# Reordering the opening loads of an attention-and-FFN block, with the second tile's statistics on ScalarE and half the keys turned late

## The chip, the cores and the metric

The kernel runs on one core of a Trainium2 chip. The metric is the device time of one execution in microseconds (us).

## The reference

One block of a transformer whose layernorms are modulated by a conditioning vector `c` (S = 2048 tokens, D = 1024, 32 query heads and 4 key heads of 128, 512 keys, then a gated FFN of width 3584):

```python
mod = (_silu(c) @ w_mod).reshape(c.shape[0], 6, 1, -1)
sa, ca, ga, sb, cb, gb = ...                      # six rows of 1024
h = _layernorm(x) * (1 + ca) + sa                 # scale ca, shift sa
x = x + ga * attention(h, k_cache, v_cache, wq, wo)   # last 512 keys only
h = _layernorm(x) * (1 + cb) + sb
x = x + gb * ffn(h)
```

The change touches only how the first line for `h` and the first heads of the attention get under way.

## The kernel before

TensorE, VectorE, ScalarE and GpSimd run at once and hand buffers over by semaphores that a small recorder (`T.op`) places. The opening works on the first 512 tokens (four tiles of 128) and does this: load four token tiles, the columns of `w_mod` for the scale `ca`, query weights, keys, the columns for the shift `sa`, values; normalize the tiles; transpose them on TensorE (`open_turn`), copy them out of PSUM (`open_evict`), multiply by 1 + ca (`open_scale`); project the first six heads (`q_open` for heads 0 to 3 on 256 tokens at a time, `q_more` for heads 4 and 5); turn the keys on TensorE; make the shift row from 8 x 8 one-column matmuls (`shift_column`); and from it one shift per head (`shifts`), which is added as the query leaves PSUM (`q_shifted`). Then come the scores of head 0 and the loop over heads.

The loads, as issued:

```python
for t in range(TPC): load_x(t)          # 4 x 256 KB
load_ca(0)                              # scale weights, half of the columns: 4 x 256 KB
load_wq(0, (0,))                        # query group 0, half of the rows: 512 KB
load_ca(1)
load_wq(0, (1,))
T.op(Q_k, ... k_nat ...)                # all keys: 512 KB
load_wq(1)                              # query group 1: 2 x 512 KB
load_sa()                               # shift weights: 8 x 256 KB
for gk in range(Hkv): ...               # values: 4 x 128 KB
```

The keys, and the end of the opening:

```python
def turn_keys():
    for i in range(GK):                 # 16
        b = (QBK, XBK)[i // 8]
        transpose(bank_bf(b)[...], k_nat[...], P, [B_kn], PB[b])
    for j in range(2):
        T.op(DVE, lambda: V.tensor_copy(kT[:, 8 * j:8 * j + 8, :], ...), ...)

turn_keys()
q_more(4, range(DT))                    # head 4: 8 matmuls of 512 columns
for kc in range(6):
    shift_column(kc)
    if kc > 3:
        keep_warm(1, XBK)               # a matmul whose result nobody reads
shift_column(6)
keep_warm(2, XBK)
shift_column(7)
T.op(DVE, lambda: V.tensor_copy(sa, bank(SFT, DT)), ...)
shifted_input(0)
q_more(5, range(3))
shifts([0], XBK)
q_more(5, [3])
... # shifts([1, 2]), q_more(5, 4..5), shifts([3, 4, 5]), q_more(5, 6..7), six q_shifted, eight shifted_input
scores(0)
exps(0, 2)
```

And the step of the head loop that weights the values. `between` runs after the matmuls and ahead of the reciprocal:

```python
def pv(i, between):
    for kt in range(KT):
        for j in (0, 2, 1, 3):
            mm(bank(...), ex[es][:, kt, ...], v_sb[...], ...)      # 128 x 129
    between()
    T.op(DVE, lambda: V.reciprocal(rl, den), ...)
    T.op(DVE, lambda: V.tensor_tensor(o_sb[...], num, rl_bc, ALU.mult), ...)
```

The softmax here doesn't subtract the row's maximum and nothing guards it: scores larger than these inputs give would overflow.

Of the kernel before, what the change touches and what calls it, by code (L numbers as in the profile page):

```python
# [8 lines left out]
P = 128  # L9
# [109 lines left out]
def bass_adaLN_cond__sliding_block_cached__swiglu_ffn__prompt_kernel(  # L119
# [104 lines left out]
    for i in (2, 3):  # L224
        xsum[i], B_xsum[i] = small("xsum%d" % i, 3, F32)
    shift, B_shift = small("shift", 6, F32)
    B_shift = [B_shift, _Buf("shift1"), _Buf("shift3")]
    SHIFTS = (0, 1, 1, 2, 2, 2)
# [33 lines left out]
    with nc.Block() as block:  # L262

        @block.gpsimd
        def _(g):
# [13 lines left out]
            for t in range(TPC):  # L279
                load_x(t)  # L280
# [12 lines left out]
            def load_sa():  # L293
                for kc in range(DT):
                    T.op(Q_wm[DT + kc], lambda: SP.dma_start(wm[:, DT + kc, :], w_mod[kc * P:(kc + 1) * P, 0:D]), writes=[B_sw[kc]])
# [7 lines left out]
            def load_wq(gi, halves=(0, 1)):  # L303
# [4 lines left out]
                for j in halves:  # L308
# [6 lines left out]
            load_wq(0, (0,))  # L315
            load_ca(1)
            load_wq(0, (1,))
            B_kn = _Buf("kn")
            k_nat = M.take(AT_MS * KB, [Hkv, KT * P], BF16, [B_kn])
            Q_k, Q_v = dq("q_k"), dq("q_v")  # L320
            T.op(Q_k, lambda: SP.dma_start(k_nat, A_k_cache[0, :, Sk - W:Sk, :].rearrange("g (p k) d -> p g (k d)", k=KT)),
                 writes=[B_kn])
            load_wq(1)
            load_sa()
# [9 lines left out]
            for gk in range(Hkv):  # L334
                T.op(Q_vg[gk], lambda: SP.dma_start(
                    v_sb[:, gk * KT:(gk + 1) * KT, 0:P],
                    A_v_cache[0, gk, Sk - W:Sk, :].rearrange("(p k) d -> p k d", k=KT)), writes=[B_vg[gk]])

            def hd(i):

                p = i % Hq
# [117 lines left out]
            TBK = (OBK, OBK + 1, SCB[1], OBK + 1)  # L459
# [9 lines left out]
            def scale_done(half):  # L469
# [3 lines left out]
                T.op(DVE, lambda: V.tensor_copy(g1f[:, lo:hi], g1[:, lo:hi]), reads=[B_g1h[half]], writes=[B_g1f])  # L473
# [11 lines left out]
            def open_evict(tt):  # L485
                b = TBK[tt]
                dst = h_sb[1][:, :, tt * P:(tt + 1) * P]
                src = bank_bf(b)[:, 0:DT * P].rearrange("p (a b) -> p a b", a=DT)
                if tt == 2:
                    T.op(ACT, lambda: A.activation(dst, src, AF.Copy), writes=PB[b] + [B_hn[1][tt]])  # L490
                else:
                    T.op(DVE, lambda: V.tensor_copy(dst, src), writes=PB[b] + [B_hn[1][tt]])  # L492

            def open_scale(th, kc, st=DVE):
                x_ = h_sb[1][:, kc, 256 * th:256 * th + 256]
                rd = B_hn[1][2 * th:2 * th + 2]
# [6 lines left out]
            Q0 = [SCB[0], SCB[2], SCB[3], OBK, OBK + 1, QBK]  # L503

            def q_open(i, kcs, th):

                for kc in kcs:
                    mm(bank(Q0[i], 256, 256 * th), wq_sb[0][:, kc, hd(i) * P:(hd(i) + 1) * P], h_sb[1][:, kc, 256 * th:256 * th + 256],
                       kc == 0 and th == 0, kc == DT - 1, [B_wq[0][kc // 4], B_o[th][kc]], PB[Q0[i]], loose=True)

# [19 lines left out]

            keep_warm(7)
# [3 lines left out]
            sums_1(2)  # L535
            ln_stats(1, 1, 0)
            ln_norm(0, 0, n0[0], B_n0[0])
            ln_stats(1, 1, 1)
            ln_rstd(1)
            sums_1(3)  # L540
            open_turn(0)
            open_evict(0)
            keep_warm(2)
            scale_column(0, 0)
            keep_warm(3)
            scale_column(0, 1)
            keep_warm(2)
            ln_norm(1, 1, n0[1], B_n0[1])
            sums_2(2)
            scale_column(0, 2)  # L550
            keep_warm(1)
            open_turn(1)
            open_evict(1)
            scale_column(0, 3)
            scale_done(0)
            keep_warm(2)
            sums_2(3)
            for kc in range(4):
                open_scale(0, kc)
            ln_norm(2, 2, n0[2], B_n0[2])  # L560
            q_open(0, range(4), 0)
            q_open(1, range(4), 0)
            open_turn(2)
            open_evict(2)
            ln_norm(3, 3, n0[3], B_n0[3])
            q_open(2, range(4), 0)
            q_open(3, range(4), 0)
            open_turn(3)
            open_evict(3)
            scale_column(1, 0)  # L570
            scale_column(1, 1)
            for kc in range(4):
                open_scale(1, kc, ACT if kc == 3 else DVE)
            scale_column(1, 2)
            scale_column(1, 3)
            scale_done(1)
            for i in range(4):
                q_open(i, range(4), 1)
            for th in range(2):
                for kc in range(4, 8):  # L580
                    open_scale(th, kc, ACT if kc > 5 else DVE)
            for th in range(2):
                for i in range(4):
                    q_open(i, range(4, 8), th)
# [37 lines left out]
            def turn_keys():  # L622
                for i in range(GK):
                    b = (QBK, XBK)[i // 8]
                    transpose(bank_bf(b)[:, (i % 8) * P:(i % 8 + 1) * P], k_nat[:, i // KT, (i % KT) * P:(i % KT + 1) * P], P,
                              [B_kn], PB[b])
                for j in range(2):
                    T.op(DVE, lambda: V.tensor_copy(kT[:, 8 * j:8 * j + 8, :],
                                                    bank_bf((QBK, XBK)[j])[:, 0:8 * P].rearrange("p (a b) -> p a b", a=8)),
# [968 lines left out]
```

## Time and profile before

| | before |
|---|---|
| time, median of 3 runs | 1168.09 us |
| span of the profiled execution | 1165.9 us |
| first query matmul | 12.01 us |
| last shift weight landed | 26.25 us |
| scores of head 0 | 29.83 to 30.69 us |
| weighted values of head 0 / head 4 start | 32.68 / 43.70 us |
| from the start of head 4 to the end | 1122.2 us |

The columns of the timeline are start in us, length in us, engine, source line and operation, out<-in with the form, number of instructions, and in brackets the idle time ahead and what ended it.

### The profile page before, as it was taken

What the parts mean: (1) busy time and instruction counts of PE and PEld (TensorE: products, weight loads), DVE (VectorE), ACT (ScalarE), POOL (GpSimd) and SP (SyncE); (2) the same over time, 40 slices, a digit from 0 to 9 for tenths busy, and PEclk for the clock granted to TensorE, in tenths of its full rate; (3) what the DMA queues carried; (4) which work ended last, traced back from release to release, by engine and by line L of the source; (5) the groups of instructions that cost most, each with busy time, mean ns of one, the idle gap of its engine ahead of it and who ended that gap; (6) DMA issues with size and microseconds to landing.
All of it is one profiled execution on the core that took longest, in us unless ns stands there. A gap on an engine that the chain in (4) does not pass through costs nothing.

```text
span 1165.9 us, 20810 instructions
## 1 busy us (share of the span) xinstructions
PE 1146.7 (98%) x7789; PEld 669.7 (57%) x7907; DVE 786.7 (67%) x1718; ACT 526.2 (45%) x844; POOL 21.7 (2%) x41
## 2 busy tenths in 40 slices
PE   8999999999999999999999999999999999999998
PEld 5787645777548876468864444444444444444443
DVE  4888646877638877347847688888377777776214
ACT  3777503777217775057751244444110344444110
POOL 1000000000000000000000000000010000000000
PEclk9999999999999999999999999999999999999999
DMA  9999796999859997869949765666895232322733
GB/s 289 246 250 260 203 357 231 262 272 257 268 202 284 272 218 210 306 149 287 272 99 349 247 176 182 206 180 175 276 246 179 86 86 77 105 73 65 261 126 135
DMA packets 283876, 245.57 MB, mean 211 GB/s; under 512 B 109952, under 2 KB 247168, under 8 KB 283776
## 3 DMA queue, kind: packets, MB, share of 16 engines
q1 hardware_dynamic: 253328, 179.74, 58.3%
q10 hardware_dynamic: 30448, 64.50, 15.6%
q8 instruction: 63, 1.03, 0.4%
q14 instruction: 37, 0.30, 0.1%
HBM read 189.27 MB, written 30.41 MB: 188 GB/s over the span
## 4 chain that ended last, share of the span: by engine, by line
PE 95%; DMA 2%; DVE 1%; ACT 1%; issue 1%; POOL 0%; DVEq 0%; ACTq 0%
PE ps L267 95%; DMA arena<-in_A_wo_dram 1%; ACT arena L758 1%; DMA arena<-arena 0%; PE ps L271 0%; DVE arena L775 0%; ACT arena L1025 0%; DMA arena<-in_c_dram 0%; ACT arena L742 0%; DVE arena L977 0%; DVE arena L492 0%; DVE arena L372 0%; DVE arena L707 0%; DVE arena L774 0%; DVE arena L980 0%
## 5 line engine op out<-in xcount | busy, mean ns | idle before, releaser
L267 PE MATMUL ps<-arena 128*128 128x512 bf16 (+5 forms) x7740 | 1144.3, 308 | 13.4 <-DVE arena L500 1.2
L267 PEld LDWEIGHTS ps<-arena 128*128 128x128 bf16 (+1 forms) x7858 | 666.9, 98 | 488.4 <-issue 6.8
L758 ACT ACTIVATE arena<-ps 128x1024 bf16<-128x1024 f32 x256 | 262.0, 1027 | 37.6 <-PE ps L267 34.8
L644 DVE TENSOR_TENSOR arena<-arena 128x512 f16<-128x512 bf16 (+3 forms) x510 | 223.1, 481 | 26.5 <-DMA wo_sums<-arena 13.5
L703 ACT ACTIVATE arena<-ps 128x256 f32<-128x256 f32 x180 | 68.7, 382 | 136.7 <-PE ps L267 136.2
L1304 DVE TENSOR_TENSOR arena<-ps,arena 128x512 f16<-128x512 f32 x112 | 77.3, 690 | 40.0 <-PE ps L267 37.9
L1297 ACT ACTIVATE arena<-ps 128x512 f32<-128x512 f32 x112 | 66.9, 597 | 73.6 <-PE ps L267 73.6
L707 DVE TENSOR_TENSOR arena<-ps,arena 128x256 bf16<-128x256 f32 x180 | 75.8, 421 | 32.6 <-PE ps L267 30.4
L775 DVE TENSOR_TENSOR arena<-ps,arena 128x512 bf16<-128x512 f32 x128 | 88.5, 692 | 4.5
L1326 ACT ACTIVATE ps<-ps 128x512 f32<-128x512 f32 x56 | 32.6, 582 | 119.7 <-PE ps L267 119.4
L977 DVE TENSOR_TENSOR arena<-ps,arena 128x512 f32<-128x512 f32 x34 | 23.4, 689 | 87.7 <-PE ps L267 87.6
L774 DVE RECIPROCAL arena<-ps 128x4 f32<-128x4 f32 x128 | 23.2, 181 | 52.5 <-PE ps L267 52.4
L1316 DVE TENSOR_TENSOR arena<-ps,arena 128x512 bf16<-128x512 f32 x56 | 38.6, 688 | 29.7 <-ACT arena L1311 29.7
L1311 ACT ACTIVATE arena<-ps 128x512 f16<-128x512 f32 x56 | 33.3, 595 | 31.6 <-PE ps L267 31.6
L980 DVE TENSOR_TENSOR arena<-ps,arena 128x512 bf16<-128x512 f32 x22 | 15.2, 689 | 46.0 <-PE ps L267 46.0
L428 DVE BATCH_NORM_STATS2 arena<-arena 128x6 f32<-128x512 bf16 x56 | 38.4, 687 | 9.1 <-DMA arena<-x_mid 8.8
L1008 DVE SCALAR_TENSOR_TENSOR arena<-arena 128x512 f32<-128x512 bf16 x56 | 41.6, 743 | 0.1
L1311 ACT ACTIVATE arena<-arena 128x512 f16<-128x512 f16 x56 | 34.8, 622 | 4.9 <-DVE arena L1304 4.9
L379 POOL TENSOR_TENSOR arena<-arena 128x1 f32<-128x1 f32 x30 | 19.2, 641 | 849.1 <-DVE arena L377 849.1
L929 ACT ACTIVATE arena<-ps 128x512 f32<-128x512 f32 x12 | 6.8, 596 | 60.8 <-PE ps L267 60.8
L905 DVE TENSOR_TENSOR arena<-arena 128x1024 f16<-128x1024 bf16 (+1 forms) x48 | 29.7, 686 | 6.2 <-DMA arena<-arena 6.2
L1316 DVE TENSOR_TENSOR arena<-arena 128x512 bf16<-128x512 f16 x56 | 23.8, 425 | 5.0
(61 smaller groups left out, 200.7 us busy)
## 6 DMA issues: line engine op xcount, KB each, us to landing
arena<-wo_sums ACTq DMA_DIRECT2D x46, 512.0 KB, 8.7
arena<-in_A_wq_dram SPq DMA_DIRECT2D x42, 512.0 KB, 4.9
arena<-wq_sums SPq DMA_DIRECT2D x22, 768.0 KB, 6.7
arena<-in_B_w_gate_dram SPq DMA_DIRECT2D x28, 512.0 KB, 4.2
arena<-in_B_w_up_dram SPq DMA_DIRECT2D x28, 512.0 KB, 5.4
arena<-wd_sums ACTq DMA_DIRECT2D x16, 896.0 KB, 6.6
arena<-in_A_wo_dram SPq DMA_DIRECT2D x24, 512.0 KB, 6.5
arena<-in_B_w_down_dram ACTq DMA_DIRECT2D x12, 896.0 KB, 7.4
```

What stands on the lines that cost most here:

```text
L267: T.op(PE, lambda: TE.matmul(out_ap, lhsT, rhs, start=start, stop=stop, skip_group_check=loose), reads=reads, writes=bb)
L428: T.op(DVE, lambda: V.bn_stats(st_sb[i][:, 6 * hf:6 * hf + 6], x_[:, 512 * hf:512 * hf + 512]), reads=[bx], writes=[B_st[i]])
L644: T.op(st, lambda: e.tensor_tensor(dst, x, y, op), reads=reads, writes=[dst_b])
L703: T.op(ACT, lambda: A.activation(sn[k], bank(QBK, 256), AF.Copy), writes=PB[QBK] + [B_sn[k]])
L707: T.op(DVE, lambda: V.tensor_tensor(dst, bank(XBK, 256, off), sn[k], ALU.add), reads=[B_sn[k]], writes=PB[XBK] + [B_q[i % NQ]])
L758: T.op(ACT, lambda: A.activation(ex[i % NEX][:, kt:kt + 2, :], bank(SCB[kt], 1024).rearrange("p (a b) -> p a b", a=2), AF.Exp, scale=att_s ...
L775: T.op(DVE, lambda: V.tensor_tensor(o_sb[i % NOS].rearrange("p (a b) -> p a b", a=TPC), num, rl_bc, ALU.mult), reads=[B_rl], writes=both + ...
L1008: T.op(DVE, lambda: V.scalar_tensor_tensor(acc, ms[:, kc, :], sc[:, kc:kc + 1], acc, op0=ALU.mult, op1=ALU.add), reads=[B_ms, B_sc, B_acc] ...
L1297: T.op(ACT, lambda: A.activation(fn[m][i], bank(b), AF.Copy), writes=PB[b] + [B_fn[m][i]])
L1304: T.op(DVE, lambda: V.tensor_tensor(ring[c_], bank(b), fn[m][i], ALU.add), reads=[B_fn[m][i]], writes=PB[b] + [bs[c_]])
L1311: T.op(ACT, lambda: A.activation(sl_[c_], src, AF.Silu), reads=reads, writes=writes + [B_sl[c_]])
L1316: T.op(DVE, lambda: V.tensor_tensor(dst, u_[0], s_[0], ALU.mult), reads=[s_[1]] + [x for x in u_[1:]], writes=[db] + list(bb))
```

## The change

The intent: begin the first query matmul earlier (two tiles are enough for it), give the scale weights the place of the tiles that aren't needed yet, let ScalarE take the second tile's statistics so that VectorE has only one tile to sum, and bring the shift weights forward by sending half the keys, half of query group 1 and three quarters of the values behind them. The diff, cut to its core (it also splits two evictions between VectorE and ScalarE, moves PSUM banks and takes heads 0 to 7 in plain order):

```diff
-            for t in range(TPC):
-                load_x(t)
+            load_x(0)
+            load_x(1)
             load_ca(0)
             load_wq(0, (0,))
+            load_x(2)
+            load_x(3)
             load_ca(1)
             load_wq(0, (1,))
-            ... all keys ...
-            load_wq(1)
-            load_sa()
+            load_wq1(0)                 # half of the columns: heads 4 and 5
+            load_sa(range(6))
+            load_keys(0)
+            load_sa(range(6, DT))
...
-            for gk in range(Hkv):
+            load_values(0)
+            load_wq1(1)
+            load_keys(1)                # values 1 to 3 follow query group 2
...
-            sums_1(2)                   # ScalarE: tile 2
-            ln_stats(1, 1, 0)           # VectorE: tile 1
+            sums_1(1)                   # ScalarE: tile 1; tile 2 goes to VectorE, later
...
-            turn_keys()
             q_more(4, range(DT))
-            for kc in range(6):
-                shift_column(kc)
-                if kc > 3:
-                    keep_warm(1, XBK)
+            for kc in range(3):
+                shift_column(kc)
+            q_more(5, range(3))
+            for kc in range(3, 6):
+                shift_column(kc)
+            turn_keys(0, SCB[0])        # eight of sixteen
+            q_more(5, range(3, 6))
             shift_column(6)
-            keep_warm(2, XBK)
+            q_more(5, [6])
             shift_column(7)
             T.op(DVE, lambda: V.tensor_copy(sa, bank(SFT, DT)), writes=PB[SFT] + [B_sa])
             shifted_input(0)
-            q_more(5, range(3))
+            q_more(5, [7])
...         # shifts of heads [1..5] in one group, for [1, 2] and [3, 4, 5] before
-                pv(i, mod_columns if i % 2 else lambda: None)
+                pv(i, mod_columns if i % 2 else (lambda: turn_keys(1, QBK)) if i == 0 else lambda: None)
```

The last line puts the other eight key transposes, and VectorE's copy of them, between the weighted values of head 0 and its reciprocal.

## The prediction

> **What bounds the kernel now.** I read the page first, for the bound of the whole: the chain that ended last is TensorE nearly throughout, and TensorE is busy for 98% of the span.
>
> ```profile
> PE 1146.7 (98%) x7789; PEld 669.7 (57%) x7907; DVE 786.7 (67%) x1718; ACT 526.2 (45%) x844; POOL 21.7 (2%) x41
> ...
> PE 95%; DMA 2%; DVE 1%; ACT 1%; issue 1%; POOL 0%; DVEq 0%; ACTq 0%
> ```
>
> TensorE idles 1165.9 - 1146.7 = 19.2 us in all. The change touches only the opening (first tiles, first six queries, first attention scores), so whatever it gains or loses is a shift of the moment at which the dense TensorE stream begins. Next I read the table of 1 us windows over the first 46 us: TensorE is busy 41.45 us of them, so the opening holds 4.55 us of idle time; 1.2 us of that lie before the first instruction and can't be had. Then the timeline, to see what ends each idle time:
>
> ```profile
> 6.08 1.06 ACT L516 ACTIVATE arena<-arena 128x1024 bf16<-128x1024 bf16 x1 [2.96 <-DMA arena<-in_A_x_dram]
> 7.16 0.62 PE L271 MATMUL ps<-arena 128*128 128x128 bf16 x8 [1.22 <-DVE arena L383]
> 12.01 1.22 PE L267 MATMUL ps<-arena 128*128 128x256 bf16 x8 [0.82 <-DVE arena L500]
> 16.18 5.59 PE L267 MATMUL ps<-arena 128*128 128x256 bf16 x48 [0.40 <-DVE arena L500]
> 21.60 1.06 PE L271 MATMUL ps<-arena 128*128 128x128 bf16 x16
> 22.71 9.22 PE L267 MATMUL ps<-arena 128*128 128x512 bf16 x139
> 32.24 8.07 PE L267 MATMUL ps<-arena 128*128 128x512 bf16 x71 [0.30 <-ACT arena L758]
> ```
>
> The reader is to see: ScalarE waits for the third token tile until 6.08; the first query matmul starts at 12.01 behind a VectorE scaling; from 16.18 to 31.8 TensorE has almost no gap. The 16 transposes at 21.60 are the keys, the 139 instructions at 22.71 are heads 4 and 5, the shift columns and the first scores. Last, the windows of that stretch, for the loads:
>
> ```profile
> 24.00:25.00 1.00, 1.00 (x34) 0.88 (x32) 0.00 (x0) 0.00 (x0) 0.00 (x0) 1.00 1.27 316
> 25.00:26.00 1.00, 0.92 (x30) 0.76 (x28) 0.00 (x0) 0.00 (x0) 0.00 (x0) 1.00 1.16 242
> 26.00:27.00 1.00, 1.00 (x20) 0.64 (x18) 0.04 (x1) 0.00 (x0) 0.00 (x0) 1.00 0.34 64
> ```
>
> The last column is GB/s: the opening loads end at about 26. By issue time and time to landing, the last shift weight lands at 26.25, and the matmuls on it start at 26.49. So before the change TensorE and the loads arrive together: trimming TensorE's work alone could gain only 0.24 us, trimming the loads alone nothing.
>
> **What the Trainium skill says.** "TensorE: Matmul & The Clock Gate", section "Wait - 56ns, not 53.3ns?", gives warm start-to-start times of 55.6 ns (128 columns), 215.7 ns (512) and a floor near 25 ns. The trace agrees: 56, 216 and 25 ns between starts of single records; 256 columns show 110 ns. I count work with these. "DMA: Bandwidth & Descriptors", section "Queues, rings and completion order", has descriptors consumed in ring order on each DMA engine; the landings here come in issue order, 0.75 us apart for each 256 KB, which lets me re-date them by position. "PSUM - Partial Sum Buffer", section "PSUM bank collisions raise a hardware error", wants two engines kept off one bank at once; the program's waits do that, so the two halves of a split eviction (VectorE, then ScalarE) run in series. No run yet shows this last.
>
> **The change part by part.**
>
> *Loads.* With two token tiles ahead of the scale weights, their four pieces take the landing times of before's third to sixth load: 6.05, 6.76, 7.48, 8.23 instead of 7.48 to 9.73. The first query weights land at 9.73 instead of 11.24. Half the keys (0.26 MB) and half of query group 1 (0.52 MB) go behind the shift weights: 0.79 MB at 0.35 MB per us makes the last shift weight 2.2 us earlier, about 23.8.
>
> *Second layernorm on ScalarE.* Tile 1 lands at 4.18. Sum, scale and squares took 2.66 us from 6.08 to 8.74; from 4.25 they end at 6.9. VectorE sums up by 7.45, GpSimd's power ends at 8.0, VectorE evicts tile 0 (7.84 to 8.52, as before) and normalizes tile 1 by 9.05. Turn (8 x 0.056, 0.17 to drain) to 9.72, half eviction to 10.15, first scaling, and the lag of 0.42 us from scaling start to matmul start seen before 12.01: the first query matmul at **10.6 instead of 12.01, a gain of 1.4**.
>
> *Tiles 2 and 3 come later.* Their order on VectorE now stands behind the scalings. Sixteen query matmuls end at 12.5. VectorE's statistics of tile 2 run 11.07 to 12.43, aggregate and epsilon to 12.86, power to 13.5, norm to 14.09. TensorE has two scale columns (0.2 each) and four warm-up matmuls (0.86), done at 13.76: **idle 0.4**. Turn 2, two columns and one warm-up end at 15.2. The second scale is ready at 15.58, its first scaling ends at 15.98, matmul at 16.1: **idle 0.9**. Tile 3's turn and the first token half of the queries take to 18.55, idle 0.15; 32 x 0.11 then end at 22.07. Before ended at 21.6, then turned 16 keys, and began head 4 at 22.71; now it begins at 22.15. **Gain 0.55, but with no keys turned: 0.45 for the first eight still in the opening, 0.45 for the other eight later.**
>
> *Shift weights and keys.* Head 4 (8 x 0.216), eight shift columns (0.2 each), seven of head 5 (1.5) and eight key transposes (0.55 with the switch) put the end of the last shift column near 27.65, one us later than before's 26.65. Four warm-ups (0.86) are gone. The weights have landed by 23.8: no wait.
>
> *After the shift row.* Before, six head-5 matmuls (1.3 us) and split shift groups filled the waits. Now one head-5 matmul stands there. Copy of the row to 27.95, shifts of head 0 at 28.15: **idle 0.43**. Shifts of heads 1 to 5 end at 29.5, their copy at 29.78, query 1 is evicted on VectorE by 30.6. Scores of head 0 need four banks: one free after the copy, one after query 1. They run 29.6 to 31.1 for 0.86 of work: **idle 0.9**. Before, they ran 29.83 to 30.69.
>
> *First heads.* Weighted values of head 0 start at 33.0 instead of 32.68. The other eight keys are turned there (0.5) and their copy (0.65 on VectorE) stands ahead of the reciprocal, so VectorE runs 1.1 to 1.5 us later until head 3, and head 2's weighted values start at 39.1 instead of 38.05. From then on TensorE is dense in both.
>
> *Sum.* Start of queries -1.4; one warm-up more after it, +0.2; idle from 12.5 on 0.4 + 0.9 + 0.15 + 0.43 + 0.9 and about 0.55 in heads 0 to 2, so 3.3, against before's 1.2: +2.1. That is **+0.9** on a walk whose hand-overs I can't date better than 0.1 each.
>
> **The rivals.** (1) *The loads were the bound, and the new order frees 2.2 us.* For it: landing and use 0.24 us apart, and head-5 matmuls replacing warm-ups between shift columns look like work put into a load wait. Against it: TensorE has 0.25 us of gaps between 16.6 and 29.4, so it would need to reach the shift columns earlier, and my walk brings it to head 4 only 0.55 earlier. If tile 2's norm or the second scale came 0.5 to 1 us sooner than I walk, the time would be 1166 to 1167. (2) *The hidden rival: VectorE becomes the bound in heads 0 to 3*, as it holds the moved key copy. It is at 9.1 of 10 us there already between 30 and 40. Then the lag spreads, +1.5 to +2: near 1170. (3) *Everything shifted is absorbed:* the second head's exponentials hold TensorE anyway (0.30 wait at 32.24), so some shift at 30 vanishes: 1168.
>
> **Range and chances.** The walk gives 1168.1 + 0.9 = 1169.0. I take a part off for rival 1, as the walk counts every hand-over in full: **1168.7**. Low end: rival 1 in full, 1166.0. High end: rival 2, 1170.4. Two per cent is 23 us, more than five times the idle time in the opening: a change of 2% needs something outside this stretch. Same 0.98, the others 0.01 each.
>
> **What would show it.** First query matmul near 10.6 behind a VectorE scaling; a TensorE gap near 15.2 to 16.1; ScalarE starting on tile 1 near 4.2; last shift weight near 23.8 with TensorE passing it three us later; gaps of 0.4 and 0.9 us between the shift row and the scores; head 2's weighted values near 39. Wrong, if the shift columns wait for their weights (then loads bound it), if the scores of head 0 begin before 29.5, or if windows after 45 us differ by more than the shift.

## More of the kernel before

The main lines of the page and of the timeline stand in the prediction. What it did not show is the timeline of VectorE just behind the opening.

```profile
33.79 0.18 DVE L774 RECIPROCAL arena<-ps 128x4 f32<-128x4 f32 x1 [0.74 <-PE ps L267]
34.01 0.69 DVE L775 TENSOR_TENSOR arena<-ps,arena 128x512 bf16<-128x512 f32 x1
34.62 1.41 DVE L644 TENSOR_TENSOR arena<-arena 128x1024 f16<-128x1024 bf16 x2
35.94 0.68 DVE L639 CAST arena<-ps 128x512 bf16<-128x512 f32 x1
36.54 0.17 DVE L774 RECIPROCAL arena<-ps 128x4 f32<-128x4 f32 x1
...
41.69 0.18 DVE L774 RECIPROCAL arena<-ps 128x4 f32<-128x4 f32 x1
...
44.81 0.18 DVE L774 RECIPROCAL arena<-ps 128x4 f32<-128x4 f32 x1 [0.41 <-PE ps L267]
```

Between the reciprocal of head 0 (33.79) and that of head 4 (44.81) the timeline marks no idle time in front of any instruction of VectorE.

## The result, and the profile after

The changed kernel took **1170.68 us**, the median of four runs (1170.36 to 1172.75), against 1168.59 (1167.99 to 1169.35) for the kernel before in the same rounds. The ratio is 1.0021, with a 95% interval of 1.0004 to 1.0039: the same within 2%, but slower by some two microseconds rather than by the 0.6 that was predicted, and just above the predicted range. (A ratio is the mean time of one kernel's fast runs over that of the other's fast runs of the same rounds, so it is not quite the ratio of the medians quoted.)

From the page after, the busy times and the engines of the chain that ended last:

```profile
PE 1153.8 (99%) x7904; PEld 669.2 (57%) x7904; DVE 786.0 (67%) x1716; ACT 527.7 (45%) x846; POOL 21.7 (2%) x41
...
PE 94%; DMA 3%; DVE 2%; ACT 1%; issue 0%; POOL 0%; ACTq 0%; DVEq 0%; SPq 0%
```

At first sight TensorE idles less (1169.2 - 1153.8 = 15.4 us for 19.2 before) in a longer span. That reading fails: the page before has 7789 matmuls against 7907 weight loads, the page after 7904 of each, so some hundred matmul records were missing before, and the busy sums can't be subtracted. Starting times can. The timeline of TensorE after, over the opening:

```profile
10.42 3.15 PE L267 MATMUL ps<-arena 128*128 128x256 bf16 x36 [0.50 <-DVE arena L526]
13.89 0.62 PE L271 MATMUL ps<-arena 128*128 128x128 bf16 x8 [0.32 <-DVE arena L404]
...
15.94 1.03 PE L267 MATMUL ps<-arena 128*128 128x256 bf16 x8 [0.84 <-DVE arena L526]
...
25.86 3.62 PE L267 MATMUL ps<-arena 128*128 128x512 bf16 x70
29.66 0.39 PE L267 MATMUL ps<-arena 128*128 128x512 bf16 x1 [0.19 <-DVE arena L1125]
30.45 3.27 PE L267 MATMUL ps<-arena 128*128 128x512 bf16 x26 [0.40 <-DVE arena L1098]
33.56 0.61 PE L271 MATMUL ps<-arena 128*128 128x128 bf16 x8
34.01 8.33 PE L267 MATMUL ps<-arena 128*128 128x512 bf16 x72
42.54 5.64 PE L267 MATMUL ps<-arena 128*128 128x256 bf16 x52 [0.21 <-DVE arena L665]
```

The first query matmul is 1.59 us earlier (10.42 for 12.01). Two new waits, 0.32 and 0.84, stand at turn 2 and at the second scale. Two more, 0.19 and 0.40, stand among the four matmuls of the scores of head 0: the first of these is the last instruction of the line at 25.86 and starts at 29.10, the others at 29.66, 30.45 and 30.68. By the weighted values of head 0 the two kernels are level: 32.65 for 32.68. The late key transposes are the line at 33.56, and at 42.54 TensorE waits for VectorE. The same stretch of VectorE's timeline after:

```profile
34.21 0.69 DVE L655 COPY arena<-ps 128x1024 bf16<-128x1024 bf16 x1 [1.19 <-PE ps L271]
34.82 0.17 DVE L800 RECIPROCAL arena<-ps 128x4 f32<-128x4 f32 x1
35.02 0.69 DVE L801 TENSOR_TENSOR arena<-ps,arena 128x512 bf16<-128x512 f32 x1
...
37.55 0.17 DVE L800 RECIPROCAL arena<-ps 128x4 f32<-128x4 f32 x1
...
42.71 0.18 DVE L800 RECIPROCAL arena<-ps 128x4 f32<-128x4 f32 x1
...
45.82 0.18 DVE L800 RECIPROCAL arena<-ps 128x4 f32<-128x4 f32 x1 [0.41 <-PE ps L267]
```

The key copy is the line at 34.21. It waits for the transposes and pushes the reciprocal of head 0 from 33.79 to 34.82, which is 1.03 later. VectorE has no idle time from there to head 4, so each later reciprocal is late by the same amount: 1.01 at 37.55, 1.02 at 42.71, 1.01 at 45.82. TensorE takes this lag over in steps. Its weighted values start, from the records of the two traces:

| head | before | after | difference |
|---|---|---|---|
| 0 | 32.68 | 32.65 | -0.03 |
| 1 | 35.31 | 35.77 | +0.46 |
| 2 | 37.95 | 38.51 | +0.56 |
| 3 | 40.58 | 41.25 | +0.67 |
| 4 | 43.70 | 44.71 | +1.01 |

The first +0.46 is the eight transposes themselves (33.56 to 34.01). The rest, 0.55, comes in steps of 0.10, 0.11 and 0.34. In the last of them the timeline names VectorE (0.21 us at 42.54); that the smaller steps are waits for VectorE too is inferred, as the records of pipelined matmuls overlap and hide short waits. From head 4 on the difference stays between 1.01 and 1.09 until about 243 us.

So 1.0 us of the loss is ahead of head 4 in this pair of traces. The two profiled spans, however, differ by 3.3 us, and the other 2.3 come after head 4. The first of it is seen in TensorE's timeline at 248, after:

```profile
235.79 11.63 PE L267 MATMUL ps<-arena 128*128 128x129 bf16 x113
247.88 0.61 PE L267 MATMUL ps<-arena 128*128 128x256 f16 x4 [0.46 <-DVE arena L670]
249.12 13.12 PE L267 MATMUL ps<-arena 128*128 128x256 bf16 x133 [0.63 <-DVE arena L733]
```

Those waits stand behind a load of stored weight sums that landed at 247.01, where the trace before has it at 244.45. Before, TensorE runs through the same stretch:

```profile
235.67 24.48 PE L267 MATMUL ps<-arena 128*128 128x512 bf16 x240
260.77 1.45 PE L267 MATMUL ps<-arena 128*128 128x256 bf16 x19 [0.63 <-DVE arena L707]
```

Whether the change delays such loads, or whether they land late in some executions of either kernel, one trace of each can't tell. That, the keys and the clock became the questions of the experiments.

### The profile page after: what moved, and what is told of

Read it like the earlier page. It is cut to its first block, busy times and chain, and to the rows that moved or that the text cites. A ratio compares the mean times of both kernels' runs of the same rounds, so it can differ in the third digit from the quotient of the medians.

```text
span 1169.2 us, 20925 instructions
## 1 busy us (share of the span) xinstructions
PE 1153.8 (99%) x7904; PEld 669.2 (57%) x7904; DVE 786.0 (67%) x1716; ACT 527.7 (45%) x846; POOL 21.7 (2%) x41
## 3 DMA queue, kind: packets, MB, share of 16 engines
q10 hardware_dynamic: 30448, 64.50, 15.4%
q8 instruction: 63, 1.03, 0.4%
## 4 chain that ended last, share of the span: by engine, by line
PE 94%; DMA 3%; DVE 2%; ACT 1%; issue 0%; POOL 0%; ACTq 0%; DVEq 0%; SPq 0%
PE ps L267 93%; DMA arena<-in_A_wo_dram 1%; DMA arena<-in_B_w_down_dram 1%; DMA arena<-wq_sums 1%; ACT arena L784 0%; PE ps L271 0%; DVE arena L801 0%; DVE arena L393 0%; DMA arena<-arena 0%; ACT arena L1051 0%; ACT arena L768 0%; DVE arena L733 0%; DVE arena L1003 0%; DVE arena L1331 0%; ACT L381 0%
## 5 line engine op out<-in xcount | busy, mean ns | idle before, releaser
L267 PE MATMUL ps<-arena 128*128 128x129 bf16 (+5 forms) x7855 | 1151.4, 308 | 9.9 <-DVE arena L733 1.5
L733 DVE TENSOR_TENSOR arena<-ps,arena 128x256 bf16<-128x256 f32 x180 | 75.8, 421 | 31.7 <-PE ps L267 29.5
L400 POOL TENSOR_TENSOR arena<-arena 128x1 f32<-128x1 f32 x30 | 19.2, 641 | 852.1 <-DVE arena L398 852.1
L1343 DVE TENSOR_TENSOR arena<-arena 128x512 bf16<-128x512 f16 x56 | 23.8, 424 | 5.0
```

The lines of the kernel that those rows point to most:

```text
L267: T.op(PE, lambda: TE.matmul(out_ap, lhsT, rhs, start=start, stop=stop, skip_group_check=loose), reads=reads, writes=bb)
L733: T.op(DVE, lambda: V.tensor_tensor(dst, bank(XBK, 256, off), sn[k], ALU.add), reads=[B_sn[k]], writes=PB[XBK] + [B_q[i % NQ]])
L1343: T.op(DVE, lambda: V.tensor_tensor(dst, u_[0], s_[0], ALU.mult), reads=[s_[1]] + [x for x in u_[1:]], writes=[db] + list(bb))
```

## The experiments

The theory after the first reading: the late key copy costs 1.0 us, because it stands in front of a VectorE that has no slack until head 4. Its rivals: the shift itself is not passed on to the end; the change also costs something after the opening; and the dropped warm-up matmuls cost something. In the tables of numbers, "head 4" is the start of its weighted values in the run's trace, and "rest" is the time from there to the end.

### Copies of both kernels

Edit: none. Copies of the kernel before and of the changed one ran in the same places as the experiments, on four chips.

> The kernel before once more, unchanged, for a second trace of it. All theories: ratio 1.000 within 0.001. What it tells apart is in the trace: if the late waits of TensorE (near 247, 607 to 610, 625 and 643 us of the two traces there are) are fixed, they stand at the same places with the same lengths within 0.1 us, and 20 marks of the two traces of before differ by under 0.1 us throughout. If they are a matter of each execution, the two traces of the same kernel drift apart by 0.5 us or more after 200 us.

> The changed kernel once more, unchanged. Shift of head 4's weighted values against before: 1.01 us again under every theory (it comes from instructions in order, not from loads). Theory A (the change costs 1.0 us in the first five heads, all beyond is the luck of late loads): the time is 1 to 1.5 us over before and the wait of 1.4 us near 247 us is absent or of another length in this trace. Theory B (the change itself makes the loads of the second token chunk late): the wait near 247 us is there again with 1.1 to 1.4 us, and the time is 2.0 to 2.5 us over before.

> A third trace of the kernel before. From head 4's values to the end its two traces took 1122.2 and 1122.2 us. If late loads differ by execution alone, this one is within 1121 to 1125 too, like all other kernels' (1121.4 to 1125.6 without a clock drop). No execution at a mean clock of 0.998.

> A third trace of the changed kernel, and five more executions. Clock at 0.998 in one to three of them (theory H). From head 4's values to the end: 1122.4 to 1124.5 in its two traces; the instructions are the same as before's there, so the mean over traces should be that of before if nothing of the change acts after the opening.

> An unchanged copy of before: ratio 1.000 to 1.0012 as in its two other runs; from head 4 to the end 1122 to 1124 us; no execution with a stretch at 0.5.

> An unchanged copy of the changed kernel: 1.0 to 1.6 us over null_before3 (1.0 for the moved keys, 1.7 in the third or so of the executions where the clock falls). If it is 2 us or more over null_before3, something of the change acts after the opening, and its stretch from head 4 to the end should be over before's in this trace too.

> An unchanged copy of the kernel before: ratio 1.000 to 1.001, head 4 at 43.7 to 44.5.

| run | median us (range, runs) | ratio to the kernel before [95%] | head 4 | rest |
|---|---|---|---|---|
| null_before | 1168.77 (1168.33 to 1171.85, 6) | 1.0008 [0.9994, 1.0022] | 44.51 | 1122.2 |
| null_before2 | 1169.45 (1168.73 to 1170.97, 5) | 1.0011 [0.9998, 1.0023] | 43.83 | 1123.6 |
| null_before3 | 1169.88 (1167.95 to 1170.23, 5) | 1.0005 [0.9993, 1.0017] | 44.38 | 1124.0 |
| null_before4 | 1167.97 (1167.23 to 1169.91, 6) | 0.9992 [0.9974, 1.0011] | 43.78 | 1121.8 |
| null_after | 1170.26 (1168.55 to 1177.93, 6) | 1.0025 [1.0003, 1.0047] | 46.65 | 1122.4 |
| null_after2 | 1170.72 (1169.13 to 1171.32, 5) | 1.0018 [1.0005, 1.0030] | 46.42 | 1122.5 |
| null_after3 | 1170.50 (1169.77 to 1172.03, 5) | 1.0015 [1.0003, 1.0027] | 44.84 | 1123.1 |

Four things follow. First, the yardstick: unchanged copies come out at 0.9992 to 1.0011, so a median of three to six runs is good to about one microsecond and no better. The 22 runs of the copies of before have a mean of 1169.09, the 16 of the changed kernel 1170.81, or 1170.34 without the single run of 1177.93. But the kernel before also ran 53 times beside the experiments, as the yardstick of the ratios, and these runs have a mean of 1168.68. With the first rounds included, the means are 1168.79 (79 runs) and 1170.88 (20 runs, or 1170.50 without that one): the change costs 1.7 to 2.1 us, and by the copies alone 1.3 to 1.7.

Second, the rest. Over all traces, the first pair included, it is 1122.8 for the five of before (1121.8 to 1124.0) and 1123.1 for the four of after (1122.4 to 1124.5). The two means are 0.3 apart and the executions of one kernel 2.1 to 2.2. So the 2.3 us after head 4 in the first pair of traces are the scatter of executions, not the change: the rest of the first copy of the changed kernel is 1122.4, and its TensorE does not wait at 248. Its timeline of that stretch is one line:

```profile
235.81 26.54 PE L267 MATMUL ps<-arena 128*128 128x512 bf16 x267
```

Third, something new: head 4 of the changed kernel is at 44.7 to 44.8 in two traces and at 46.4 to 46.7 in the other two. The windows of about 3.4 us of null_after show why. The columns are the window, its length, busy time (and number) of PE, PEld, DVE, ACT and POOL, the granted TensorE clock, the busy share of the DMA engines and GB/s:

```profile
24.10:27.50 3.40, 3.35 (x75) 2.55 (x72) 0.69 (x1) 0.00 (x0) 0.00 (x0) 1.00 0.46 126
27.50:30.90 3.40, 2.19 (x53) 1.57 (x52) 2.34 (x9) 1.66 (x3) 0.00 (x0) 1.00 0.22 58
30.90:34.30 3.40, 3.40 (x9) 1.22 (x8) 2.41 (x7) 2.31 (x4) 0.00 (x0) 0.50 1.11 337
34.30:37.70 3.40, 3.40 (x34) 2.14 (x32) 1.52 (x4) 2.11 (x3) 0.00 (x0) 0.99 1.10 327
```

The clock fell to half from 30.9 for one window, right behind a window in which TensorE was busy for 2.19 of 3.40 us, and that with one-column matmuls mostly. (This trace has 119 matmul records fewer than the first one after. One of 512 columns near 29.4, which that one has at 29.10, is among the missing, so about 2.6 us is nearer the truth.) In the first trace after, the clock stays at 1.00 until its last work is done. Half a clock for 3.41 us takes 0.0015 off the mean clock of an execution of 1169 us. The clock also falls once behind the last work of any kernel, which takes up to 0.0008 in the traces. So of the mean clocks, which are given to three places, 1.000 says that there was no drop, 0.998 that there was one, and 0.999 leaves it open. 0.998 stands in 6 of the 20 executions of the changed kernel and of its copies, in none of the 22 of the copies of before, and in one (1173.09 us) of the 53 runs of before beside the experiments; none of before's five traces has a drop.

Why only some executions? In null_after the drop (30.93) and the fall behind the last work (1167.57) start 333.0 steps of 3.413 us apart, and the drops of the other traces lie a whole number of such steps ahead of that fall too. So there is a grid in time, and it lies differently against the program in each execution. In null_after and null_after2 one step of it covers 27.51 to 30.93 and 27.04 to 30.46; by my count of the columns streamed, the array was at work for 0.16 and 0.14 of it. In the two traces of the changed kernel without a drop the grid has its edges at 28.17 and 28.77, the thin stretch falls into two steps, and the lowest share is 0.45 and 0.38. This is worked out from the times in the traces; no run placed the grid on purpose.

Fourth, where the loss lies. Averaged over the traces, head 4 starts at 44.04 in the five of before and at 45.66 in the four of after: 1.6 later, which is 0.7 in the two traces without a drop and 2.5 in the two with one. The first pair's +1.01 is one draw of this. Before's own opening varies because TensorE waits for the shift weights in two of its five traces, null_before and null_before3, where the last of them lands at 27.24 and 27.11 instead of 26.25 and head 0 starts at 33.49 and 33.36. From null_before:

```profile
26.60 6.15 PE L267 MATMUL ps<-arena 128*128 128x1 bf16 x83 [0.28 <-DMA arena<-in_w_mod_dram]
```

No trace of the changed kernel waits for its shift weights.

### pad_before: a plain shift of the opening

```diff
             q_shifted(5, DVE)
+            keep_warm(5, XBK)
             scores(0)
```

> The kernel before with five idle warm-up matmuls (5 x 0.2155 = 1.08 us) just ahead of the first scores: the opening's loads, VectorE's and ScalarE's work and the order of heads stay as before, only TensorE's stream is shifted by about what the change shifts it. Head 4's weighted values: +1.0 (0.9 to 1.1). Theory A (late waits are luck) and theory C (any such shift passes through): the time is 1.0 us over before within 0.6. Theory D (a shift of TensorE against the stream of loads makes later loads late): 2.0 us or more, with a wait near 247 us in the trace. Theory B (the load order or the head order of the change does it): 1.0, and no wait near 247.

Measured: 1170.95 us (1168.59 to 1171.98), ratio 1.0017 [1.0003, 1.0031]. Head 4 starts at 45.60, 1.09 later than in null_before of the same chip, and the five runs' mean is 1.2 above that copy's (1.9 above that of the runs of before in the same rounds). A delay of 1.09 that is put into the opening by hand comes out at the end, within the scatter: no sign that anything later absorbs it. (The prediction's third rival, that a shift is absorbed, falls here.)

### before_keys_late: the late keys alone

The kernel before, with only the second eight keys turned in head 0:

```diff
-            turn_keys()
+            turn_keys(0)
...
-                pv(i, mod_columns if i % 2 else lambda: None)
+                pv(i, mod_columns if i % 2 else (lambda: turn_keys(1)) if i == 0 else lambda: None)
```

> The kernel before with one other piece alone: the second eight keys are turned in head 0, between its values and their reciprocal. Theory K (moved keys cost what the changed kernel loses): head 0's values 0.1 to 0.45 us earlier (the shift weights' landing limits what the 0.45 us of transposes taken away can give), head 1's 0.45 later than that, and by head 4 another 0.5 later behind VectorE: 0.5 to 0.9 us over before of a like opening. If VectorE has slack there: head 4 at -0.1 to +0.1.

Measured: 1170.53 us (1169.10 to 1170.89), ratio 1.0015 [1.0001, 1.0028]. Heads 0 to 4 start at 32.68, 35.79, 38.53, 41.28 and 44.74: with one part of the change alone, +1.04 at head 4 (0.5 to 0.9 was expected), by the steps of the changed kernel. Its TensorE timeline:

```profile
22.11 3.30 PE L267 MATMUL ps<-arena 128*128 128x512 bf16 x56
25.76 6.17 PE L267 MATMUL ps<-arena 128*128 128x1 bf16 x83 [0.35 <-DMA arena<-in_w_mod_dram]
32.23 1.51 PE L267 MATMUL ps<-arena 128*128 128x512 bf16 x18 [0.30 <-ACT arena L757]
33.58 0.61 PE L271 MATMUL ps<-arena 128*128 128x128 bf16 x8
34.03 8.33 PE L267 MATMUL ps<-arena 128*128 128x512 bf16 x71
42.57 3.68 PE L267 MATMUL ps<-arena 128*128 128x256 bf16 x35 [0.21 <-DVE arena L638]
```

The last two lines are those of the changed kernel to 0.03 us. The second is what became of the saving: eight transposes less brought TensorE to the shift columns 0.6 earlier, and there it waited 0.35 for their weights, which were still in the old order. Head 0 starts at 32.68 as before.

### keys_early: the changed kernel with all keys in the opening

```diff
             load_keys(0)
+            load_keys(1)
             load_sa(range(6, DT))
...
             for kc in range(3):
                 shift_column(kc)
+            turn_keys(0, SCB[0])
             q_more(5, range(3))
             for kc in range(3, 6):
                 shift_column(kc)
-            turn_keys(0, SCB[0])
+            turn_keys(1, SCB[0])
...
-                pv(i, mod_columns if i % 2 else (lambda: turn_keys(1, QBK)) if i == 0 else lambda: None)
+                pv(i, mod_columns if i % 2 else lambda: None)
```

> The changed kernel with all keys loaded ahead of the last two shift weights and all 16 turned in the opening, none between head 0's values and their reciprocal. If the copy of the moved keys on VectorE is what delays heads 2 to 4 (0.55 us of the 1.01), then head 0's values come at +0.4 to +0.5 (the eight transposes now stand there), and head 4's also at +0.4 to +0.5: the lag stops growing, and the time is 0.5 to 0.6 us under the changed kernel's. If the growth has another cause (ScalarE's exponentials, the later second weight group), head 4 is at +0.9 to +1.0 as in the changed kernel.

Measured: 1169.39 us (1168.37 to 1170.26), ratio 1.0009 [0.9996, 1.0021]; the changed kernel's copy on the same chip 1.0025. The distance from head 0 to head 4 tells the keys apart from everything else, as the clock drops end before the weighted values of head 0 begin:

| keys turned | kernels | head 0 to head 4 |
|---|---|---|
| all in the opening | before and its four copies, pad_before, before_nowarm, before_loads, interleaved and its repetition, keys_early, keys_warm, keys_warm_col | 11.01 to 11.02 us |
| half in head 0 | after and its three copies, after_warm, before_keys_late | 12.06 to 12.07 us |

There is no exception in 19 traces, whatever the load order and the clock: behind the start of head 0 the late keys cost **1.04 us**. Put back, they cost again in the opening; keys_early had the half clock too (from 30.4), so its head 4 at 45.57 says little, and the next runs were to take that away.

### before_nowarm: do the four warm-ups keep the clock?

```diff
             for kc in range(6):
                 shift_column(kc)
-                if kc > 3:
-                    keep_warm(1, XBK)
             shift_column(6)
-            keep_warm(2, XBK)
             shift_column(7)
```

> The kernel before without its four warm-ups between the shift columns. TensorE's work falls by 0.86 us there, but the last shift weights land at 26.3 to 27.3, so the columns wait for them. Theory H: the array has less to stream in one stretch of 3.4 us; [...]one or more executions at 0.998, and time equal or worse than before. Theory L: no execution at 0.998, time 0 to 0.3 us under before.

Measured: 1168.19 us (1167.41 to 1175.87), ratio 1.0009 [0.9989, 1.0029]. Four of six runs lie between 1167.41 and 1168.32, the other two at 1175.87 and 1170.74, and these two alone have mean clocks of 0.997 and 0.996. The trace is of the first of the two, and its windows show the drop:

```profile
26.00:29.40 3.40, 2.58 (x54) 1.78 (x52) 0.94 (x4) 0.49 (x1) 0.00 (x0) 1.00 0.36 75
29.40:32.80 3.40, 3.40 (x33) 1.61 (x31) 3.28 (x11) 1.55 (x3) 0.00 (x0) 0.50 0.47 161
```

Removing four matmuls whose results nobody reads brought a drop, by the mean clocks, to two of six executions of the kernel before, which otherwise shows one for certain in 75. A second drop, at 879 us, lies far from the edit and is not explained. So the warm-ups between the shift columns seem to help to keep the clock. But the window ahead of this drop also holds waits of 0.51 and 0.30 us for shift weights, the last of which landed at 27.34, so late loads are a rival that this one trace can't exclude. And the warm-ups are not all of it: before_keys_late has them, with less work for TensorE ahead of them, and one of its five executions has 0.998. Four of six runs here are at the low end of what copies of before take, so where the clock holds there may be something in leaving them out; six runs don't show it.

### after_warm and keys_warm: three warm-ups put back

The changed kernel, and keys_early, each with

```diff
             q_more(5, [7])
+            keep_warm(1, SCB[0])
...
+            keep_warm(2, SCB[0])
             scores(0)
```

> The changed kernel with three warm-up matmuls put back into waits: one between the last head-5 matmul and the shift groups, two between the shift groups and the first scores. Theory H (the opening of the changed kernel leaves the array so little to stream around 27 to 31 us that the granted clock falls to 0.5 for one stretch of 3.4 us, as the second trace of it shows): no execution has a mean clock of 0.998, the trace shows no stretch at 0.5 after 8 us, head 4's weighted values stand 1.0 us over before's of a like opening, and the time is 0.5 to 1.2 us under the changed kernel's (1170.3 to 1170.7), as the clock falls in a third to two thirds of its executions and costs 1.7. Theory L (late loads alone make the rest of the loss): clock as before in some executions at 0.998, time as the changed kernel's within 0.3 us.

> All keys turned in the opening and the same three warm-ups. Theory H: no execution at 0.998, no stretch at 0.5; head 4's values 0.2 to 0.6 us over those of the first trace of before; time 1168.3 to 1169.0, equal to before within 0.5 us. If the warm-ups do not keep the clock: as keys_early, 1169.4 with some executions at 0.998.

The clock did as hoped: four of five executions of each have a mean of 1.000 and the fifth 0.999, and in the trace of after_warm the stretch in question stays at 1.00:

```profile
26.20:29.70 3.50, 3.50 (x73) 2.20 (x71) 1.99 (x7) 0.69 (x1) 0.00 (x0) 1.00 0.02 6
29.70:33.10 3.40, 2.98 (x18) 1.29 (x17) 3.37 (x9) 3.30 (x5) 0.00 (x0) 1.00 0.90 303
```

The time did not. after_warm took 1171.08 us (1169.99 to 1171.54), ratio 1.0017 [1.0004, 1.0030], where 0.5 to 1.2 us less than the changed kernel was expected: a miss. keys_warm took 1169.63 (1168.24 to 1171.86), 1.0011 [0.9999, 1.0023]. For keys_warm 1168.3 to 1169.0 was expected, so this is a miss too. Without the drop, head 4 starts at 44.88 in the first (44.71 after) and at 44.41 in the second. By one trace of each, the keys back in the opening are thus worth 0.47 of their 1.04, as 0.58 is paid again ahead of head 0.

A drop costs 1.6 to 1.9 us at head 4 (46.42 and 46.65 against 44.71 and 44.84). At six executions in twenty or more this is an estimated 0.5 us or more in the mean. But the runs do not show it in the time: among the executions of the changed kernel and its copies the six with 0.998 have a mean of 1170.75, and the five with 1.000, without the run of 1177.93, 1170.35; and after_warm is not faster. That the clock drops is shown; how much of the loss it makes is not.

### keys_warm_col: a scale column moved ahead of the second wait

```diff
             scale_column(1, 1)
+            scale_column(1, 2)
             rows_done(2)
             open_evict(2, ACT)
-            scale_column(1, 2)
-            keep_warm(1, QBK)
             scale_column(1, 3)
```

> keys_warm with the third scale column taken ahead of tile 2's transposes and two warm-ups' worth of waiting removed there: the second scale is ready 0.4 us earlier, so the wait of 0.84 us ahead of the fifth query step falls to 0.4 to 0.5 and everything behind it moves 0.3 to 0.4 us forward. Time 0.3 to 0.4 us under keys_warm, 0.2 to 0.5 under before, if the column was what the wait was for; if the wait grows elsewhere (tile 3's normalization or eviction), no gain.

Measured: 1170.99 us (1169.40 to 1171.12), ratio 1.0015 [1.0003, 1.0027]. The wait grew to 1.17 us and ended at 16.03. The first scaling was done at 15.52 as hoped, but the query weights of the fifth step landed at 15.98 only (15.69 in the first trace after), so the load ended the wait. And with one more warm-up gone the clock fell here, at 16.2; head 4 starts at 45.66. An attempt that failed twice.

### before_loads and interleaved: what the part about the shift columns is worth

before_loads takes from the change that half of query group 1 goes behind the shift weights, with heads 0 to 7 in plain order. interleaved also puts head 4's matmuls between the shift columns, in the place of the four warm-ups; all keys stay in the opening.

```diff
-            load_wq(1)
+            load_wq1(0)
             load_sa()
+            load_wq1(1)
```

```diff
-            q_more(4, range(DT))
-            for kc in range(6):
+            for kc in range(DT):
+                q_more(4, [kc])
                 shift_column(kc)
-                if kc > 3:
-                    keep_warm(1, XBK)
-            shift_column(6)
-            keep_warm(2, XBK)
-            shift_column(7)
```

> The kernel before with one piece of the change alone: half of query group 1 (0.52 MB) is loaded behind the shift weights instead of ahead of them (this needs heads 5 and 6 in plain order). The last shift weight lands 1.4 us earlier, near 24.9 to 25.8 instead of 26.25 to 27.2. In the first trace of before nothing waited for it, in the later ones of before TensorE waited 0.3 to 0.5 us. So: no wait for shift weights in the trace; head 4's values at 43.7 to 43.9 (first trace of before 43.70, second 44.51); time 0.2 to 0.6 us under before, if the late landings are usual; equal to before if they are not.

> A version meant to beat both: before_loads (half of query group 1 behind the shift weights, all keys early), with the eight shift columns interleaved with head 4's eight matmuls and the four warm-ups dropped. TensorE has 0.86 us less to do ahead of the shift row, the shift weights land by 25.2 to 26, and every stretch of 3.4 us keeps 512-column work in it. Head 4's values at 43.0 to 43.3 in a trace without a late start (before 43.70), no stretch at 0.5 after 8 us; time 0.4 to 0.7 us under before, which the rounds can only just show. If the columns wait for weights again, head 4 at 43.5 to 43.7 and no gain.

> Same source as interleaved. Theory (putting head 4's matmuls between the shift columns gains in the opening, and the rest passes it on): median 0.5 to 1.5 us below the copy of the kernel before in this batch, weighted values of head 4 at 42.8 +- 0.3 in the trace. Rival (nothing gained: the four warm-ups dropped bring clock drops, as the slow run of 1173.34 may have been): a mean within 0.4 us of the copy, with mean clocks of 0.998 or less in one or more executions.

before_loads took 1168.40 us (1167.62 to 1168.92), ratio 1.0000 [0.9987, 1.0012]. The last shift weight landed at 25.19 instead of 26.25, and head 4 started at 43.71, as in the first trace of before, in which nothing waited for these weights either. Against the two copies in which TensorE waited (44.51 and 44.38) the same trace is 0.7 to 0.8 earlier. One trace can't tell whether the new order keeps such waits away, and the median doesn't show a gain.

interleaved took 1167.29 us (1166.71 to 1173.34), ratio 0.9996 [0.9979, 1.0013]; its repetition on another chip 1168.63 (1166.66 to 1170.36), 0.9994 [0.9977, 1.0012]. The TensorE timeline of interleaved:

```profile
22.69 8.37 PE L267 MATMUL ps<-arena 128*128 128x1 bf16 x135
31.36 12.86 PE L267 MATMUL ps<-arena 128*128 128x512 bf16 x123 [0.30 <-ACT arena L766]
```

There is no wait from 22.69 to the exponentials, and the wait for these begins 0.88 earlier than before. Head 4 starts at 42.82, and in the repetition at 42.69, against 43.70 to 44.51 in before and its copies. Ten of the twelve executions have a mean clock of 1.000, the other two 0.999. In the traces this is the best opening. In the time it is not shown: the twelve runs have a mean of 1168.43 against 1169.09 of before's copies and 1168.68 of its 53 other runs, with both intervals across 1, and the copy of before in the repetition's own batch had the lower median. The repetition's trace has a rest of 1125.3, the copy's 1121.8, and that swallows the 1.09 it had won by head 4. I do not claim that it beats the kernel before.

## Why the prediction was wrong, and where it was right

**In short.** The walk to head 4 came out (+0.9 walked, +1.01 in the first pair of traces); the step that failed is the one from the walk to the time, "1168.1 + 0.9" less "a part off for rival 1". It took off 0.3 that the runs don't give back, started from a base of 1168.1 where 79 runs of the kernel before have a mean of 1168.79, and had no term for the halved clock, which puts head 4 1.6 to 1.9 us later in two of four traces of the changed kernel. The change costs 1.7 to 2.1 us; how the part above 1.0 divides stays open.

**Right: the walk through the opening.** The first query matmul was to come at 10.6 and came at 10.42; ScalarE began tile 1 at 4.19 (4.25). The waits were to be 0.4 and 0.9 at turn 2 and the second scale: 0.32 and 0.84. Head 4's queries began at 21.84 (22.15), the last shift column ended near 27.3 (27.65), the last shift weight landed at 24.25 and nobody waited for it (23.8 was predicted, though 26.25 - 2.2 is 24.05). The two halves of tile 1's split eviction ran one behind the other, 9.52 to 9.94 on VectorE and from 9.98 on ScalarE, as the walk had it. Two readings were off without harm: the scale weights did not take over before's landing times but landed at 4.88 to 7.82 (6.05 to 8.23), and tile 0's eviction was at 8.05 in the trace before, not at 7.84.

**Wrong in the walk: "After the shift row".** The waits there were counted too high: 1.33 was predicted, and the 1 us windows from 27 to 31 hold 0.84. The scores of head 0 were to run from 29.6 and by the records began at 29.10, which is one of the prediction's own signs of being wrong ("before 29.5"): the records of the shifts of heads 1 to 5 end at 28.98 and not at 29.5. Head 0's weighted values came at 32.65, not at 33.0.

**Right in kind, in sum by luck: VectorE as the bound in heads 0 to 3.** The sum of the walk, +0.9, was +1.01 at head 4 in the first pair, but two errors cancel in it. Up to head 0 the change is level (-0.03, where +0.3 was walked). Behind it the walk went from +0.3 to +0.9, and the late half of the keys added 1.04: 0.46 of transposes and the lag of VectorE. The lag also spread more slowly than walked: head 2's weighted values started at 38.51, not at 39.1, and the last third of it came at head 4. before_keys_late shows the 1.04 alone. The second rival, "VectorE becomes the bound in heads 0 to 3", describes what happened, with +1.0 where it put +1.5 to +2.

**Wrong: "I take a part off for rival 1".** The first rival had the loads as the bound. In the trace that the prediction read they were not: before_loads has them 1.06 us earlier, and its head 4 is within 0.01 of that trace. In two of the four copies they were, with waits of 0.28 and 0.39 us, so "trimming the loads alone nothing" holds for one execution and not for all. The new order may save these waits, but the changed kernel's time shows nothing of it: it lies above the 1169.0 and not below.

**Wrong: "The walk gives 1168.1 + 0.9", with a high end at 1170.4.** The base was the median of three runs. All 79 later runs of the same kernel have a mean of 1168.79, and medians of five or six unchanged copies lie between 1167.97 and 1169.88. With this base and the measured +1.0 the walk would have ended at 1169.8, against 1170.50 to 1170.88 for all runs of the changed kernel. The 0.7 to 1.1 left is of the size of the estimated 0.5 or more for the clock, which the times don't show by themselves. The range was built from mechanisms alone and had no term for the scatter of a median, which is about one microsecond either way and as large as everything the walk added up.

**Missing: the clock, at "Four warm-ups (0.86) are gone".** In the kernel before, taking them away went with drops of the clock in two of six runs, against one for certain in 75 with them; in the changed kernel at least six of twenty executions have such a drop, at 1.6 to 1.9 us by head 4. The walk had no line for that. That this moved the median is not shown, as said above.

**Right on average: the rest passes everything on.** Rest is 1122.8 before and 1123.1 after. For a single execution it moves by more than 2 us, so the first pair of traces, 3.3 us apart, showed about twice the change. The prediction's sign for this, windows after 45 us that differ by more than the shift, was met in that pair, but by the scatter of executions; with only that pair I would have blamed late loads.

**Open.** Why the weight sums and other late loads land up to some microseconds apart in executions of one kernel; which share of the loss is the clock's; and whether interleaved is faster.

## What to carry to other kernels

Before moving work out of an opening, look at the engine it lands on: eight transposes and one copy of 0.69 us, moved to where VectorE had no idle time for 11 us, cost 1.04 us in each of six traces. What they gave back where they had been was nothing in one kernel (before_keys_late) and about 0.6 in the other (keys_warm against after_warm). A matmul that computes nothing may still be holding the clock, so judge its removal by the clock of several executions and not by its length. And where the expected effect is a thousandth of the time, run unchanged copies of both kernels first, and compare when a fixed point of the program starts in the traces before comparing medians.

## What the Trainium skill lacked or had wrong

- "TensorE: Matmul & The Clock Gate", section "Part 1: The HAM clock gate (the "warmup" mystery)", has the clock throttled after at least one idle window of about 3.4 us. Here it fell to 0.50 behind a window in which the profile has TensorE busy for about 2.6 of 3.40 us (null_after, a missing record added), or for 2.58 of 3.40 (before_nowarm). Most of these instructions were matmuls of one column. By my count of the columns streamed, the array was at work for 0.14 to 0.36 of the windows ahead of the five drops counted (a missing record would add 0.06 in three of them); windows with 0.33 to 0.50 elsewhere had no drop, so the runs give no clean threshold. That page also tells of a clock that oscillates when TensorE pauses often and shortly, but gives no share of busy time for it. The length of the half-clock stretch, 3.41 us, agrees with the 3413 ns of that page.
- The same page has the semaphore increments of small tiles run one behind the other, but doesn't tell how a chain of one-column matmuls on the whole array ends. The records of 48 of them start 25 ns apart (27.62 to 28.81 us in the changed kernel), but their completions, which the next engine waits for, came 34 ns apart (27.81 to 29.42), so that VectorE's copy behind them began at 29.44, while by the records the last of them had ended at 28.98.
- No page gives a figure for how far executions of one whole kernel scatter where loads are tight: from the fifth head to the end, 1121.8 to 1124.0 us in five traces of the kernel before, and ratios of 0.9992 to 1.0011 for unchanged copies against it.
